# Placing matmul operands modulo 256 bytes, and key-span copies on GpSimd instead of VectorE

## The chip, the cores and the metric

The kernel runs on one core of one Trainium2 chip. The metric is the device time of one execution in microseconds. PE is TensorE's matmul side and PEld its weight load, DVE is VectorE, ACT is ScalarE, POOL is GpSimd, and SP is the engine that issues most DMAs.

## The reference

Three parts follow each other. Chunked attention: 4 batches, 8 heads, 768 tokens, head size 64; each chunk of 32 queries sees 8 memory keys and a span of 56 keys around it. Then a top-1 mixture of 8 experts (512 to 1024 to 512) over the 3072 tokens, and then a dense SiLU layer (512 to 2048 to 512).

```python
k_full = np.concatenate([mem_k, k_ctx], axis=2)          # 8 + up to 56 keys
scores = scale * np.matmul(q_c, k_full.transpose(0, 1, 3, 2))
a = np.exp(scores)                                       # scores less their row maximum
a = a / (np.sum(a, axis=-1, keepdims=True) + 1e-09)
out[:, :, c_start:c_end] = np.matmul(a, v_full)
...
expert_idx = np.argmax(logits, axis=1)
h = np.maximum(x[mask] @ w1[e], 0.0)
out[mask] = gate_w[mask, None] * (h @ w2[e])
...
h = x @ w_in
g = h * (1.0 / (1.0 + np.exp(-h)))
return (g @ w_out).astype(np.float32)
```

## The kernel before

**Products.** Expert and dense products run on the fp32r type, each operand split into a high and a low tile, so one product is three matmuls (`three`, lines 94 to 98): high times high, high times low, low times high. In each, one operand is loaded into the array as 128 columns (stationary; its load shows as PEld) and the other streams past it (moving, 256, 384 or 512 columns). While one matmul streams, the weights of the next are loaded.

**Attention** runs over 16 pairs of heads in 32 units of half a pair each (loop from line 895). A unit `u` has, on PE, the scores of unit u (24 matmuls of 32 x 128), the transposes of the exponents of u-1 (`turned`), the transposes of the output of u-3 (`columns`), and the values of u-2 (24 matmuls of 32 x 130). On DVE it has the row maximum (`mx`, line 795), the subtraction (`e`, line 798), the key spans of one head (line 714), and the division (`den` at 832 and 834, `xb` at 836). ACT has the exponentials, three copies, and squares. Between these, one step at a time, DVE takes the steps of a routing generator (`advance`, lines 296 to 330). Each engine works its instructions in the order in which they are written.

The key spans are what `windows(j, h, part)` writes: it lays the 56-key span of each of 12 chunks out in `kbuf[j % 2]` (64 partitions, 12 x 56 elements, line 714), and the 8 memory keys beside them (12 x 8 elements, line 715). Head 0 of a pair goes on ACT, head 1 on DVE; the memory keys go on POOL from pair 3 on. The scores of pair j wait for them. Pair 0 is laid out ahead of the loop, pair j+1 while pair j is worked on. POOL begins with fills of buffers and, at line 276 to 290, the constants of the routing (`routing_constants`), and these are written ahead of the first unit.

**Slots.** Tokens of one expert are worked on in slots: two leading slots of two tiles of 128 tokens (`pre`), up to four of three tiles (`threes`), and then as many of two tiles as there are (`twos`). For each of 8 column blocks of the expert, `first_mm` does 12 matmuls with w1 stationary and the slot's x moving (256 columns for two tiles, 384 for three), and `second_mm` does 3 matmuls for each tile, with h stationary and the block of w2 (called v2, 512 columns) moving. The leading slots have their x and h in the small space (tiles `xhs`, `hhs`), all others in the large space (`xhl`, `xhm`, `hhl`). In this run 3 three-tile and 8 two-tile slots are taken after the leading two.

**Dense layer.** Six groups of 512 tokens, 16 column blocks each. `up` does 12 matmuls with w_in stationary and the group's y moving; `add` does 12 with the gated g stationary and w_out moving. The weights of blocks 0 to 5 are in `w2a`, of 6 to 15 in `w2b`, both as high and low tiles. Groups 0, 2, 4 have y in `yh`, `yl`; groups 1, 3, 5 in `yh1`, `yl1`. The profile leaves numbers out of names, so `yh` stands for both.

**Places.** Pools are stacked from both ends of a partition's memory. The built program gives these start addresses, modulo 256 bytes (all inner offsets that the matmuls use are multiples of 256 bytes):

| tiles | before | after |
|---|---|---|
| expert weights w1, v2 | 224 | 224 |
| x, h of the small space | 160 | 160 |
| x, h of the large space | 224 | 160 |
| w2a | 160 | 224 |
| w2b, g, y of groups 1, 3, 5 | 224 | 224 |
| y of groups 0, 2, 4 | 128 | 224 |

Of the kernel before, what the change touches and what calls it, by code (L numbers as in the profile page):

```python
# [10 lines left out]
F32 = mybir.dt.float32  # L11
F32R = mybir.dt.float32r
# [10 lines left out]
P = 128  # L23
# [10 lines left out]
DM = H * D  # L34
KD = DM // P
# [11 lines left out]
N2 = (N - 2 * SLOT - NE) // SLOT + NE  # L47
SURE2 = (NTC - 3 * N3 + 1) // 2
NA = 2 * N2

LEAST = 2.0 ** -15

# [5 lines left out]
def tile_chunk_attention_top1_moe_silu_mlp(ctx, tc, qT, kT, vW, emb, tau, wm, wo, out, dbg=None):  # L58
    nc = tc.nc
    wo = wo.bitcast(I32)  # L60
    PE, ACT, DVE, POOL, SP = nc.tensor, nc.scalar, nc.vector, nc.gpsimd, nc.sync
# [8 lines left out]
    gd = dram.tile([N, 1], F32, name="gd")  # L70
    td = dram.tile([NA * P, 1], I32, name="td")
    bank = [psum.tile([P, DM], F32, name=f"bank{i}") for i in range(8)]
# [5 lines left out]
    d = const.tile(full, F32, name="d")  # L78
# [5 lines left out]
    rows3_i = const.tile([P, 3 * (N3 + 1)], I32, name="rows3_i")  # L84
    rows2_i = const.tile([P, NA], I32, name="rows2_i")
    chosen_i = const.tile([1, 2], I32, name="chosen_i")
# [143 lines left out]
    seg = rp.tile([P, NE, NT], F32, name="seg")  # L230
    tiles = rp.tile([P, 1, NA], F32, name="tiles")
    mx = rp.tile([P, NT, 1], F32, name="r_mx")
# [29 lines left out]
    wideh = rp.tile([P, NTC, 2 * NE], F32, name="wideh")  # L262
    ahf = rp.tile([P, NT, NA], BF16, name="ahf")
    ah = rp.tile([P, NT, 2, NA], BF16, name="ah")
    ixs = rp.tile([P, NA + 3 * N3], F32, name="ixs")
    ixp = rp.tile([P, NA], F32, name="ixp")
# [414 lines left out]
    with ExitStack() as a:  # L681
# [26 lines left out]
        def windows(j, h, part):  # L708
            rows = slice(h * D, h * D + D)
            half = slice(part * (NCH // 2), (part + 1) * (NCH // 2))  # L710
            src, dst = kraw[j][rows], kbuf[j % 2][rows, h, half]
            copy = DVE.tensor_copy if h else ACT.copy
            w = src[:, NMEM + half.start * CH:]
            copy(dst[:, :, NMEM:], bass.AP(tensor=w.tensor, offset=w.offset, ap=[w.ap[0], [CH, NCH // 2], [1, WIN]]))
            (POOL.tensor_copy if j > 2 else copy)(
                dst[:, :, 0:NMEM], src[:, 0:NMEM].unsqueeze(1).to_broadcast([D, NCH // 2, NMEM])
            )
# [36 lines left out]
        for part in range(2):  # L754
            for h in range(2):
                windows(0, h, part)
# [139 lines left out]
        for u in range(NU + 2):  # L896
# [12 lines left out]
            if ahead < NJ:  # L909
                windows(ahead, 1, u % 2)  # L910
                windows(ahead, 0, u % 2)
                advance()
# [48 lines left out]
    lg = ex.enter_context(tc.tile_pool(name="lg", bufs=1, side="right"))  # L961
    large = [space(lg, "l", 3)]
    large.append(dict(large[0], x=tuple(lg.tile([P, KD, 3 * P], F32R, name=f"x{n}m") for n in "hl")))
    yfirst = [lg.tile([P, 2, DM], F32, name=f"yfirst{n}") for n in range(2)]
    w2d = tuple(lg.tile([P, DM], F32R, name=f"v2{n}3") for n in "hl")
    for n, s in enumerate(order):
        s.y = lambda n=n: yfirst[n] if n < 2 else ymore[:, 0:order[n].nt]
# [18 lines left out]
                advance(pe=True)  # L986
    rt.close()
    ypool = ctx.enter_context(tc.tile_pool(name="ypool", bufs=1))
    ymore = ypool.tile([P, 4, DM], F32, name="ymore")
    POOL.memset(ymore, 0.0)  # L990


# [9 lines left out]
    GT2 = TG * P  # L1002
    NG = NT // TG
    yrow = ctx.enter_context(tc.tile_pool(name="yrow", bufs=1))
    yr = [y[:, c] for y in yfirst for c in range(2)]
    tok_i = [yrow.tile([P, TG], I32, name=f"tok{g}") if g else pre_i for g in range(NG)]
    gt = [yrow.tile([P, TG], F32, name=f"gt{i}") for i in range(2)]
    yt = [tuple(yrow.tile([P, KD, GT2], F32R, name=n) for n in ("yh", "yl"))]

    dx = ctx.enter_context(ExitStack())  # L1010
    dp = dx.enter_context(tc.tile_pool(name="dp", bufs=1))
# [87 lines left out]
    j = 0  # L1099
# [13 lines left out]
    for s in plan:  # L1113
        for at, do in sorted(plan[s], key=lambda p: p[0]):
            f = int(at)
# [25 lines left out]
    with ExitStack() as a:  # L1141
# [73 lines left out]
        for i in range(NI2):  # L1215
            g, f = steps[i]
            j = NB2 + i
# [89 lines left out]
```

## Time and profile before

| | us |
|---|---|
| median of 3 runs (1033.83 to 1038.53) | 1034.95 |
| the profiled execution | 1034.16 |
| its span, first to last instruction | 1032.2 |
| PE busy | 985.2 (95%) |
| PEld busy | 822.4 (80%) |
| DVE busy | 613.6 (59%) |
| ACT busy | 463.2 (45%) |
| POOL busy | 168.6 (16%) |

The stages are read from the first matmul of each: attention up to about 115 us, the slots to 474 us, the dense layer to the end. A matmul's duration in the timeline is modelled and overlaps its neighbour's; the distance of two starts is the time that one really takes up. The chain of waits of this profile holds only the last output transfer and is of no use here.

### The profile page before, as it was taken

The numbers are of one execution on the slowest core, as the hardware profiler recorded it, in microseconds if no ns is written. First come the engines' busy times: TensorE is split into PE (matmuls) and PEld (weight loads), VectorE is DVE, ScalarE is ACT, GpSimd is POOL, SyncE is SP. The second block draws the span as 40 slices with busy tenths as digits, with TensorE's granted clock in tenths as the row PEclk, the third lists the DMA queues.
The fourth block names the chain that finished last, engine by engine and source line by source line (L and its number), as shares of the span: only waits on it lengthen the run. The fifth ranks groups of instructions, "written<-read, shape, count | busy, mean of one in ns | idle before, by whom it ended". The sixth has DMA issues, their size and how long they took to land. (4 is left out here: it accounts for less than half of the span.)

```text
span 1032.2 us, 16833 instructions
## 1 busy us (share of the span) xinstructions
PE 985.2 (95%) x6366; PEld 822.4 (80%) x6366; DVE 613.6 (59%) x1225; ACT 463.2 (45%) x890; POOL 168.6 (16%) x225
## 2 busy tenths in 40 slices
PE   6888888999999999998999999999999999999998
PEld 4666677999888999997778888878887888788886
DVE  8999797677777887896899942422232232223221
ACT  8886555445456565664544333222321331232221
POOL 5133032011020000002230002050023005001001
PEclk9999999999999999999999999999999999999999
DMA  8986756566488887776343201020011002000001
GB/s 302 341 316 231 244 196 208 196 216 224 130 272 255 273 276 256 253 242 191 95 124 100 82 1 41 19 64 1 1 52 30 1 4 79 1 1 31 10 1 41
DMA packets 44213, 139.37 MB, mean 135 GB/s; under 512 B 6422, under 2 KB 6480, under 8 KB 44120
## 3 DMA queue, kind: packets, MB, share of 16 engines
q1 hardware_dynamic: 36632, 118.22, 33.7%
q0 software_dynamic: 7488, 19.95, 6.4%
q8 instruction: 53, 0.87, 0.4%
q14 instruction: 40, 0.33, 0.1%
HBM read 115.32 MB, written 22.84 MB: 134 GB/s over the span
## 5 line engine op out<-in xcount | busy, mean ns | idle before, releaser
L1169 DVE TENSOR_TENSOR sg<-bank,sg 128x512 f32<-128x512 f32 x96 | 66.2, 690 | 235.9 <-ACT sg L1164 235.9
L1164 ACT ACTIVATE sg<-bank 128x512 f32<-128x512 f32 x96 | 57.4, 598 | 277.7 <-PE bank L98 244.2
L96 PE MATMUL bank<-yh,w2bh 128*128 128x512 f32 x240 | 95.0, 396 | 0.0
L92 DVE TENSOR_TENSOR gl<-sg,gh 128x512 fp32r<-128x512 f32 x92 | 63.8, 693 | 52.5 <-ACT gh L91 48.5
L98 PE MATMUL bank<-yh,w2bl 128*128 128x512 f32 x240 | 94.5, 394 | 0.0
L97 PE MATMUL bank<-yl,w2bh 128*128 128x512 f32 x240 | 94.3, 393 | 0.0
L97 PE MATMUL bank<-w2bl,gh 128*128 128x512 f32 x224 | 87.4, 390 | 0.0
L96 PE MATMUL bank<-w2bh,gh 128*128 128x512 f32 x224 | 87.4, 390 | 0.0
L98 PE MATMUL bank<-w2bh,gl 128*128 128x512 f32 x224 | 87.4, 390 | 0.0
L91 ACT CAST gh<-sg 128x512 fp32r<-128x512 f32 x92 | 57.1, 621 | 64.8 <-DVE sg L1169 60.9
L1192 POOL DMA_INDIRECT out_dram<-o,tok x20 | 20.4, 1022 | 389.0 <-DVE o L1189 348.4
L181 ACT ACTIVATE hhl<-bank 128x256 fp32r<-128x256 f32 (+1 forms) x88 | 36.3, 413 | 101.0 <-PE bank L98 95.2
L96 PE MATMUL bank<-v2h,hhl 128*128 128x512 f32 x200 | 80.4, 402 | 0.0
L97 PE MATMUL bank<-v2l,hhl 128*128 128x512 f32 x200 | 78.9, 394 | 0.0
L98 PE MATMUL bank<-v2h,hll 128*128 128x512 f32 x200 | 78.5, 393 | 0.0
L92 DVE TENSOR_TENSOR w1l<-raw,w1h 128x512 fp32r<-128x512 f32 x106 | 72.9, 687 | 8.4 <-ACT w1h L91 5.3
L92 DVE TENSOR_TENSOR v2l<-raw,v2h 128x512 fp32r<-128x512 f32 x106 | 72.9, 688 | 0.0
L182 DVE SCALAR_TENSOR_TENSOR hll<-bank,hhl 128x256 fp32r<-128x256 f32 (+1 forms) x88 | 40.3, 458 | 54.6 <-ACT hhl L181 53.7
L147 POOL DMA_INDIRECT xrowl<-xd,rows_i x28 | 31.0, 1108 | 243.1 <-PE bank L169 201.2
L97 PE MATMUL bank<-xll,w1h 128*128 128x256 f32 (+1 forms) x224 | 68.5, 306 | 2.1 <-DVE xll L92 2.1
L96 PE MATMUL bank<-xhl,w1h 128*128 128x256 f32 (+1 forms) x224 | 68.7, 307 | 1.4 <-DVEq L1134 1.4
L98 PE MATMUL bank<-xhl,w1l 128*128 128x256 f32 (+1 forms) x224 | 68.7, 306 | 0.2 <-DVE w1l L92 0.2
(308 smaller groups left out, 2426.9 us busy)
## 6 DMA issues: line engine op xcount, KB each, us to landing
raw<-in_wm_dram SPq DMA_DIRECT2D x109, 512.0 KB
coded<-in_wo_dram SPq DMA_DIRECT2D x36, 512.0 KB
vbuf<-in_vW_dram SPq DMA_DIRECT2D x32, 390.0 KB
k<-in_kT_dram SPq DMA_DIRECT2D x16, 400.0 KB
q<-in_qT_dram SPq DMA_DIRECT2D x16, 384.0 KB
xd<-xb SPq DMA_DIRECT2D x8, 768.0 KB
ys<-ymore SPq DMA_DIRECT2D x8, 512.0 KB
ys<-yfirst SPq DMA_DIRECT2D x7, 512.0 KB
```

The source lines that it names most:

```text
L91: ACT.copy(hi, src)
L92: eng.tensor_tensor(lo, src, hi.bitcast(F32), op=ALU.subtract)
L96: PE.matmul(out, lhsT=lh, rhs=rh, start=start, stop=False)
L97: PE.matmul(out, lhsT=lh, rhs=rl, start=False, stop=False)
L98: PE.matmul(out, lhsT=ll, rhs=rh, start=False, stop=stop)
L147: POOL.indirect_dma_start(out=s.where["row"][:, c], out_offset=None, in_=xd[0:LEAD * P] if s in pre else xd, in_offset=IndirectOffsetOnAxi ...
L181: ACT.activation(hh, h, AF.Relu)
L182: DVE.scalar_tensor_tensor(hl, h, 0.0, hh.bitcast(F32), op0=ALU.max, op1=ALU.subtract)
L1164: ACT.activation(sg, h, AF.Sigmoid)
L1169: DVE.tensor_tensor(sg, h, sg, op=ALU.mult)
L1192: POOL.indirect_dma_start(out=out, out_offset=IndirectOffsetOnAxis(ap=tok_i[g][:, c:c + 1], axis=0), in_=o, in_offset=None,)
```

## The change

Three edits go to where tiles lie, one to which engine does a copy.

- `yfirst0` gets 16 more columns (64 bytes) than it uses. It lies above the large space in a pool that is stacked downward, so the large space's x, h and gather tiles move 64 bytes down.
- `ymore` gets 64 bytes more as well, and `yt[0]` (`yh`, `yl`) is allocated ahead of the small tiles `tok` and `gt` instead of behind them. This moves `w2a` by 64 bytes and `yh`, `yl` to the end of `w2a`. The table above has the result.
- In `windows`, head 1 of pairs 1 to 15 goes to POOL in place of DVE: 30 copies of 64 x 12 x 56, and 4 of 64 x 12 x 8 for pairs 1 and 2. Pair 0 stays on DVE.

```diff
--- before.py
+++ after.py
@@ -47,6 +47,8 @@
 N2 = (N - 2 * SLOT - NE) // SLOT + NE
 SURE2 = (NTC - 3 * N3 + 1) // 2
 NA = 2 * N2
+
+HOME = 16
 
 LEAST = 2.0 ** -15
 
@@ -709,7 +711,7 @@
             rows = slice(h * D, h * D + D)
             half = slice(part * (NCH // 2), (part + 1) * (NCH // 2))
             src, dst = kraw[j][rows], kbuf[j % 2][rows, h, half]
-            copy = DVE.tensor_copy if h else ACT.copy
+            copy = (POOL.tensor_copy if j else DVE.tensor_copy) if h else ACT.copy
             w = src[:, NMEM + half.start * CH:]
             copy(dst[:, :, NMEM:], bass.AP(tensor=w.tensor, offset=w.offset, ap=[w.ap[0], [CH, NCH // 2], [1, WIN]]))
             (POOL.tensor_copy if j > 2 else copy)(
@@ -961,7 +963,10 @@
     lg = ex.enter_context(tc.tile_pool(name="lg", bufs=1, side="right"))
     large = [space(lg, "l", 3)]
     large.append(dict(large[0], x=tuple(lg.tile([P, KD, 3 * P], F32R, name=f"x{n}m") for n in "hl")))
-    yfirst = [lg.tile([P, 2, DM], F32, name=f"yfirst{n}") for n in range(2)]
+    yfirst = [
+        lg.tile([P, 2 * DM + HOME * (1 - n)], F32, name=f"yfirst{n}")[:, 0:2 * DM].rearrange("p (c d) -> p c d", c=2)
+        for n in range(2)
+    ]
     w2d = tuple(lg.tile([P, DM], F32R, name=f"v2{n}3") for n in "hl")
     for n, s in enumerate(order):
         s.y = lambda n=n: yfirst[n] if n < 2 else ymore[:, 0:order[n].nt]
@@ -986,7 +991,7 @@
                 advance(pe=True)
     rt.close()
     ypool = ctx.enter_context(tc.tile_pool(name="ypool", bufs=1))
-    ymore = ypool.tile([P, 4, DM], F32, name="ymore")
+    ymore = ypool.tile([P, 4 * DM + HOME], F32, name="ymore")[:, 0:4 * DM].rearrange("p (c d) -> p c d", c=4)
     POOL.memset(ymore, 0.0)
 
 
@@ -1002,10 +1007,10 @@
     GT2 = TG * P
     NG = NT // TG
     yrow = ctx.enter_context(tc.tile_pool(name="yrow", bufs=1))
+    yt = [tuple(yrow.tile([P, KD, GT2], F32R, name=n) for n in ("yh", "yl"))]
     yr = [y[:, c] for y in yfirst for c in range(2)]
     tok_i = [yrow.tile([P, TG], I32, name=f"tok{g}") if g else pre_i for g in range(NG)]
     gt = [yrow.tile([P, TG], F32, name=f"gt{i}") for i in range(2)]
-    yt = [tuple(yrow.tile([P, KD, GT2], F32R, name=n) for n in ("yh", "yl"))]
 
     dx = ctx.enter_context(ExitStack())
     dp = dx.enter_context(tc.tile_pool(name="dp", bufs=1))
```

The order of PE, ACT and SP is the same as before. Two places on the others:

POOL, from its last constant to the first spans of the attention loop; `kbuf1`, `k3` are the spans and keys of pair 3 (odd pairs use `kbuf1`). Before:

```order
L289 MEMSET hot_132 128x192
L290 MEMSET ixs_179 128x46
L715 COPY kbuf1_204<-k3_316 64x12x8 x4
L715 COPY kbuf0_203<-k4_412 64x12x8 x4
L715 COPY kbuf1_204<-k5_516 64x12x8 x4
```

After:

```order
L291 MEMSET hot_132 128x192
L292 MEMSET ixs_179 128x46
L716 COPY kbuf1_204<-k1_222 64x12x56
L717 COPY kbuf1_204<-k1_222 64x12x8
L716 COPY kbuf1_204<-k1_222 64x12x56
L717 COPY kbuf1_204<-k1_222 64x12x8
L716 COPY kbuf0_203<-k2_239 64x12x56
L717 COPY kbuf0_203<-k2_239 64x12x8
```

The spans of pairs 1 and 2 now stand behind the constants in POOL's order.

DVE, units 12 and 13 of the attention; `mx12` is the row maximum of unit 12, `den10` the divisor of unit 10. Before:

```order
L795 TENSOR_REDUCE mx12_860<-bank0_69 128x6
L798 TENSOR_TENSOR e12_862<-bank0_69,mx12_860 128x3x2x64
L303 SCALAR_TENSOR_TENSOR r_v_130<-d_83,down_126 128x48
L714 COPY kbuf1_204<-k7_722 64x12x56
L832 TENSOR_SCALAR den10_892<-bank4_73 128x6
L305 TENSOR_REDUCE r_mv_131<-r_v_130 128x6
L834 RECIPROCAL den10_892<-den10_892 128x6
```

After:

```order
L797 TENSOR_REDUCE mx12_860<-bank0_69 128x6
L800 TENSOR_TENSOR e12_862<-bank0_69,mx12_860 128x3x2x64
L305 SCALAR_TENSOR_TENSOR r_v_130<-d_83,down_126 128x48
L834 TENSOR_SCALAR den10_892<-bank4_73 128x6
L307 TENSOR_REDUCE r_mv_131<-r_v_130 128x6
L836 RECIPROCAL den10_892<-den10_892 128x6
```

The copy between `e` and `den` is gone, and nothing else has moved.

## Rows read from the trace of the kernel before

**Rows 1.** stages: us, busy PE, PEld, DVE, ACT, POOL, PEclk, DMA, GB/s
```profile
20.00:100.00 80.00, 70.01 (x1478) 52.99 (x1476) 72.71 (x206) 62.95 (x138) 22.39 (x61) 1.00 0.87 306
115.00:474.00 359.00, 347.89 (x2144) 311.87 (x2142) 283.36 (x587) 207.16 (x423) 46.04 (x45) 1.00 0.69 228
474.00:1032.00 558.00, 544.40 (x2384) 441.07 (x2384) 230.07 (x369) 169.25 (x286) 82.63 (x84) 1.00 0.13 41
```

**Rows 2.** timeline, PE, dense: start us, us, engine, line, operation, tiles
```profile
770.63 0.39 PE L96 MATMUL bank<-w2ah,gh 128*128 128x512 f32 x1
...
773.43 0.40 PE L96 MATMUL bank<-yh,w2ah 128*128 128x512 f32 x1
...
794.97 0.39 PE L96 MATMUL bank<-w2bh,gh 128*128 128x512 f32 x1
...
797.69 0.39 PE L96 MATMUL bank<-yh,w2bh 128*128 128x512 f32 x1
...
900.76 0.40 PE L96 MATMUL bank<-yh,w2bh 128*128 128x512 f32 x1
...
903.57 0.39 PE L96 MATMUL bank<-w2bh,gh 128*128 128x512 f32 x1
```

**Rows 3.** timeline of PE, two-tile slots: a small-space one, then a large-space one
```profile
133.92 0.28 PE L96 MATMUL bank<-xhs,w1h 128*128 128x256 f32 x1
...
135.29 0.39 PE L96 MATMUL bank<-v2h,hhs 128*128 128x512 f32 x1
...
136.67 0.28 PE L96 MATMUL bank<-xhs,w1h 128*128 128x256 f32 x1
...
338.06 0.28 PE L96 MATMUL bank<-xhl,w1h 128*128 128x256 f32 x1
...
339.49 0.40 PE L96 MATMUL bank<-v2h,hhl 128*128 128x512 f32 x1
...
340.89 0.60 PE L1081 MATMUL bank<-ident,yfirst 128*128 128x128 f32 x4
```

**Rows 4.** timeline of PE, a three-tile slot
```profile
234.43 0.33 PE L96 MATMUL bank<-xhl,w1h 128*128 128x384 f32 x1
...
236.54 0.39 PE L96 MATMUL bank<-v2h,hhl 128*128 128x512 f32 x1
```

**Rows 5.** groups by line, PE, 174:474 us: xcount, busy us, mean ns
```profile
L96 PE MATMUL bank<-v2h,hhl 128*128 128x512 f32 x200 | 80.4, 402 | 0.0
...
L98 PE MATMUL bank<-xhl,w1l 128*128 128x384 f32 x96 | 32.4, 337 | 0.0
```

**Rows 6.** timeline of PE and DVE, one attention unit without a routing step
```profile
28.30 0.87 PE L821 MATMUL bank<-vbuf,et 128*32 128x130 f32 x24
28.33 0.56 DVE L798 TENSOR_TENSOR e<-bank,mx 128x384 f32<-128x384 f32 x1
...
28.92 0.51 DVE L714 COPY kbuf<-k 64x672 f32<-64x672 f32 x1
...
29.46 0.16 DVE L832 TENSOR_SCALAR den<-bank 128x6 f32<-128x6 f32 x1
```

**Rows 7.** waits, 10:112 us: who, for whom, us in total, times, longest
```profile
DVE den L832 <- PE bank L821: 4.0, 7, 1.8
```

**Rows 8.** timeline of DVE, an attention unit with a routing step
```profile
47.91 0.51 DVE L714 COPY kbuf<-k 64x672 f32<-64x672 f32 x1
48.45 0.17 DVE L832 TENSOR_SCALAR den<-bank 128x6 f32<-128x6 f32 x1
```

**Rows 9.** timeline of DVE and POOL, units 2 and 30, and POOL's last constant
```profile
13.97 0.56 DVE L795 TENSOR_REDUCE mx<-bank 128x6 f32<-128x384 f32 x1
...
14.47 0.14 POOL L290 MEMSET ixs<- 128x46 f32 x1
...
101.70 0.54 DVE L795 TENSOR_REDUCE mx<-bank 128x6 f32<-128x384 f32 x1
```

**Rows 10.** groups by line, POOL, whole span: xcount, busy us, mean ns
```profile
L281 POOL COPY row<-token 128x1 f32<-128x1 f32 x1 | 0.2, 184 | 0.1
...
L715 POOL COPY kbuf<-k 64x96 f32<-64x96 f32 x52 | 14.5, 279 | 45.6 <-DMA k<-in_kT_dram 22.5 <-PE bank L809 9.5 <-PE bank L821 4.3
```

## The prediction, made before the changed kernel ran

> **What bounds the kernel now.** I read the stages first [rows 1]. From 115 us on PE is busy 348 of 359 us in the slots and 544 of 558 in the dense layer, while DVE has 79% and 41%, at a granted clock of 1.00. What makes one matmul shorter there shortens the run by as much. In the attention (20 to 100 us) DVE has 72.7 of 80 us (91%), PE 70.0, ACT 62.9 and POOL 22.4: DVE sets the pace, and POOL has room.
>
> A busy PE is not PE at its peak, so I then read distances of starts in the timeline. All of these are runs of 12 (or 6) matmuls with nothing in between.
>
> - Dense, `add` on w2a: 770.63 to 773.43, 2.80 us for 12, **233.3 ns** each. `add` on w2b, 24 us later, same shape, same g: 794.97 to 797.69, **226.7 ns**. `up` with y of group 4 (`yh`) on w2b: 900.76 to 903.57, 234.2 ns [rows 2]. By the table of places, the operands of the 226.7 run lie 0 bytes apart modulo 256, those of the others 64 and 96.
> - Slots of two tiles, 256 columns: in the small space (x 64 bytes off w1) 133.92 to 135.29, **114.2 ns**; in the large space (in line) 338.06 to 339.49, **119.2 ns**. Their second layer, six of 512 columns: 230.0 off line, 233.3 in line [rows 3].
> - Three tiles, 384 columns, in line: 234.43 to 236.54, 175.8 ns [rows 4].
>
> So the trace holds the experiment already: distance modulo 256 goes with the pitch, 0 is best for the long runs at 512 columns, and 64 off is better at 256. The change gives each stage the relation that was the quicker one in these rows.
>
> **Dense layer.** All pairs come to 0 bytes apart, at the same remainder (224) as w2b and g have now, so I take 226.7 for all. Counts by the code: 6 groups x 12 matmuls x 6 or 10 blocks, `add` the same.
> - `add` on w2a: 432 x (233.3 - 226.7) = 2.85 us.
> - `up` on w2b, groups 0, 2, 4: 360 x 6.8 (the row gives 7.5, other runs of this class a little less) = 2.45.
> - `up` on w2a: 432 matmuls, 32 or 192 bytes off. No row here; bounded by 0 and by 6.6 each. The groups with `yh` behave as the row above (216 x 6.2 = 1.35), for the others I take 4.5 (0.95).
> - `add` on w2b after an off-line `up` starts slower than after an in-line one; half a us over 672 matmuls, and 48 last ones that read weights out of `yh`, 0.3.
>
> Sum **-8.2 us**, bounds -6.5 and -9. PE waits for nothing that this would uncover: DVE has 41% there.
>
> **Slots.** The large space comes into the relation of the small one. With 200 second-layer matmuls a term, 72 of them from the three slots of three tiles (96 first-layer ones are 32 a slot), eight slots of two tiles follow [rows 5].
> - First layer, 256 columns: 8 x 96 = 768 x (119.2 - 114.2) = 3.8 us. A run begins slower than it ends, and some runs of the small space lie nearer 115.5, so I take 4 ns: 3.1. Bounds 1.5 and 5.
> - Second layer of these: 384 x (233.3 - 230.0) = 1.3; I take 0.9. That of the three-tile slots (216) I leave at 0.2. Bounds +0.6 and -2.2 together.
> - 384 columns have no row off line. From below, the gain of the nearest row (5.0 ns, same tiles, 256 columns): 288 x 5.0 = 1.4. From above, a loss such as 64 bytes make at 512 columns (6.6 ns): 1.9. I take -0.6, nearer to the row that shares its tiles.
>
> Sum **-4.8 us**, bounds 0 and -8. DVE rises from 79% to about 80% there and stays behind PE.
>
> **Attention, what DVE loses.** 30 copies of 0.51 us. What lies beside them is the values on PE: `den` waits for both.
> - In a unit without a routing step `e` ends at 28.89, the copy stands at 28.92 to 29.43, `den` at 29.46; PE's values end at 29.17 [rows 6]. Without the copy `den` can start at about 29.24: 0.22 us a unit, and PE's values are late next.
> - Seven times `den` waits for PE's values already [rows 7]: 0 there.
> - Where a routing step stands ahead, `den` comes straight behind the copy, 47.91 to 48.45, with the values long done: the whole 0.5 [rows 8].
>
> Of the 28 copies in units 2 to 29 (told apart by the distance of their `mx` rows, the ends of which are in [rows 9]), 7 give 0, eleven stand in units without a routing step (2.4 us), ten behind one (5.0): **-7.4 us**.
>
> **Attention, what POOL gets.** The nearest rows are 279 ns for 96 elements in 12 runs and 184 ns for 1 [rows 10]: 0.99 ns an element beyond 0.18, so 672 cost 0.85 us. All of the 279 ns as per-element cost would give 1.95, the upper end. With two copies of memory keys POOL then has 1.4 us a unit (2.5 at the upper end) against 3.13 us that a unit takes ((101.70 - 13.97) / 28 [rows 9]). Its share rises, but it stays ahead. In its queue the copies now stand among the routing's `bh` steps, which wait for DVE; the spans are written two units before their use, which covers that. SP's loads of keys now wait for POOL in place of DVE, for a copy that is done two units earlier.
>
> What is not covered is the start. POOL finishes its constants at 14.61 [rows 9], and pair 1 now waits in line behind them. Its first span is done at 14.61 + 0.85 + 0.28 = 15.74, the 24 matmuls of unit 2's scores take some 0.87 (the values' row has that many [rows 6]), so unit 2's `mx` comes at 16.6 to 16.7 and not at 13.97. PE stands idle before it, and the next unit's scores want the second half behind another 1.1 us. I take **+3.0 us**, with ends 2.2 and 4.5 (POOL at its upper price).
>
> Attention together **-4.4 us**, bounds +1 and -8.
>
> **Sum.** 1034.16 (profiled) - 8.2 - 4.8 - 4.4 = 1016.8; the median lies 0.8 above the profiled run, so 1017.5. I say **1017.5 us**.
>
> **Rivals.**
> 1. *The places are not the cause.* Then w2a would be slow for another reason, and only the attention's 4.4 us remain: 1030.5. For it: the off-line dense runs differ among themselves by 2 to 4 ns, so more than the remainder acts. Against it: w2b is quick with g and slow with `yh` in neighbouring runs [rows 2], so it is the pair and not the tile. The Trainium skill ("TensorE: Matmul & The Clock Gate", Step-by-step: what each phase is for) has TensorE read moving operand and weights through two independent ports, so that loading the next weights takes nothing from the running matmul; by that rule no address would matter and this rival's time would come out. The 233.3 and 226.7 ns of one shape speak against it. Chance 0.06.
> 2. *The attention gives nothing.* The start costs 4.5 and PE's values (24 matmuls each) hold the loop, so that units without a routing step gain nothing: 0 to +2 instead of -4.4, 1022 to 1024. For it: PE has 70 of 80 us in the stage [rows 1]. Chance 0.15.
> 3. *Slower.* POOL becomes the attention's bound. A unit costs POOL the copy plus 0.56; with 3.13 us a unit now, it decides from a copy of 2.6 us on, and eats the 13 us of the other stages from about 2.85. At 3.0 us: 27 units x 0.43 + 4.5 at the start + 3 = +19, so 1035 - 13 + 19 = 1041. It would need 4.2 ns an element where the rows have 1 to 2.9. Chance 0.03.
>
> The forecast keeps 0.76.
>
> **How the numbers follow.** Ends of the forecast's own terms: attention -8 to +1, slots -8 to 0, dense -9 to -6.5; all at one end is unlikely, so about 1011 to 1024 for forecast and rival 2. With a little of rival 1's side the range is **1011 to 1025**. About 0.5% (5.2 us) is what a measurement can tell from no change. Faster by more: forecast, rival 2: 0.91. Within: rival 1, 0.06. Slower: 0.03.
>
> **What would show it.** Dense runs of `add` on w2a and `up` with any y at 227 ns. Two-tile slots' first layer at 114 to 116 ns. POOL's span copies at 0.8 to 0.9 us, DVE at some 82% of the attention in place of 91; unit 2's `mx` near 16.7; units without a routing step 0.2 us shorter, with `den` waiting for PE's values; the first expert matmul at about 111 us, not 115. I would be wrong if the 256-column pitch stayed at 119 or rose, if 384 columns rose above 178, or if the first expert matmul came at 115 or later.

## The result, and the profile after

The changed kernel takes **1025.97 us** (median, 1024.18 to 1030.07), the kernel before beside it 1035.08 us: ratio **0.9912, 95% interval 0.9894 to 0.9931**. The forecast was 1017.5 us in a range of 1011 to 1025, so the direction was right and half of the gain was missing. The same two kernels on other chips give another ratio, **0.9841 (0.9828 to 0.9854)**: 1024.00 us before, 1007.09 us after, almost all of the 17.4 us (8.2 + 4.8 + 4.4) that had been forecast. So two things have to be explained, why the sum was right there and what took some 8 us away here. In what follows A is the chip of the result, B to G are the chips of the experiments in their order (A and B may be the same one).

Profiled on A, the changed kernel took 1027.44 us, with a span of 1025.7. First the stages, as in [rows 1], moved with the earlier ends (us, busy PE, PEld, DVE, ACT, POOL, granted clock, DMA share, GB/s):

```profile
20.00:100.00 80.00, 74.19 (x1539) 56.96 (x1537) 62.39 (x191) 63.82 (x142) 38.45 (x87) 0.98 0.86 307
113.00:469.00 356.00, 345.39 (x2143) 310.23 (x2141) 282.92 (x587) 207.21 (x422) 46.00 (x45) 1.00 0.69 230
469.00:1026.00 557.00, 539.72 (x2384) 442.90 (x2384) 230.43 (x369) 169.72 (x286) 82.98 (x84) 0.99 0.13 41
```

DVE has come down from 91% to 78% of the attention (62.39 of 80 us) and POOL risen to 48%. But in the dense layer PE is busy for 4.7 us less while the stretch has hardly become shorter (557 in place of 558 us): PE stands still more.

The pitches that the forecast rests on all came. The timeline of PE on A, one `add` on w2a, one `up` of an even group on w2b, then a three-tile and a two-tile slot (start, us, engine, line, operation, tiles), which answer to [rows 2 to 4]:

```profile
770.21 0.39 PE L98 MATMUL bank<-w2ah,gh 128*128 128x512 f32 x1
...
772.93 0.39 PE L98 MATMUL bank<-yh,w2ah 128*128 128x512 f32 x1
...
896.05 0.39 PE L98 MATMUL bank<-yh,w2bh 128*128 128x512 f32 x1
...
898.77 0.39 PE L98 MATMUL bank<-w2bh,gh 128*128 128x512 f32 x1
```
```profile
228.70 0.34 PE L98 MATMUL bank<-xhl,w1h 128*128 128x384 f32 x1
...
230.78 0.39 PE L98 MATMUL bank<-v2h,hhl 128*128 128x512 f32 x1
...
332.85 0.28 PE L98 MATMUL bank<-xhl,w1h 128*128 128x256 f32 x1
...
334.23 0.39 PE L98 MATMUL bank<-v2h,hhl 128*128 128x512 f32 x1
```

Both dense runs take 2.72 us for 12, 226.7 ns each (233.3 and 234.2 before). 384 columns take 173.3 ns (175.8), 256 columns 115.0 (119.2).

The attention on A: unit 2, the last constant on POOL and the first span copy behind it, `mx` of two neighbouring units without a routing step (kernel before, then the changed one), and two rows of the waits from 10 to 110 us (who, for whom, us in total, times, longest), beside [rows 6, 7, 9]:

```profile
16.88 0.56 DVE L797 TENSOR_REDUCE mx<-bank 128x6 f32<-128x384 f32 x1 [5.26 <-PE bank L788]
```
```profile
14.09 0.14 POOL L292 MEMSET ixs<- 128x46 f32 x1
14.29 0.75 POOL L716 COPY kbuf<-k 64x672 f32<-64x672 f32 x1
```
```profile
27.68 0.55 DVE L795 TENSOR_REDUCE mx<-bank 128x6 f32<-128x384 f32 x1
30.36 0.55 DVE L795 TENSOR_REDUCE mx<-bank 128x6 f32<-128x384 f32 x1
```
```profile
27.49 0.55 DVE L797 TENSOR_REDUCE mx<-bank 128x6 f32<-128x384 f32 x1
29.95 0.55 DVE L797 TENSOR_REDUCE mx<-bank 128x6 f32<-128x384 f32 x1
```
```profile
DVE den L834 <- PE bank L823: 13.3, 22, 1.8
...
PE bank L788 <- issue: 2.0, 1, 2.0
```

POOL copies a span in 0.75 us, unit 2 begins at 16.88 us, a unit without a routing step takes 2.46 us in place of 2.68, and `den` now waits 22 times for PE's values where it waited 7 times. The last row is new and was not foreseen: once, at 54.23 us, PE stood for 2.0 us in the middle of a unit's scores, and the profile shows nothing that it waited for. Units 15 and 16 took 4.82 and 3.86 us in place of some 2.5, the second of them for the most part at a granted clock of 0.5.

Now the missing part. In the rows that follow, `gh` is the high half of the gated g that ACT makes for `add`; `held` is the copy of group 0's first sums, which frees the banks for group 1; `give` scatters a group's output rows, and `pick` and `pick_gate` gather the rows, tokens and gates of the next group, four of each. Waits of PE in the dense layer, kernel before and then the changed one (480 to 1030 us):

```profile
PE bank L96 <- ACT gh L91: 4.2, 3, 1.6
PE bank L96 <- ACT held L1184: 1.6, 1, 1.6
```
```profile
PE bank L98 <- ACT gh L93: 6.7, 3, 2.3
PE bank L98 <- ACT held L1189: 1.8, 1, 1.8
PE bank L98 <- issue: 0.5, 1, 0.5
```

These waits were there before, and they have grown. Each of the three on `gh` stands ahead of the `add` of block 5 of groups 2, 3 and 4; the one on `held` is the fourth. One of them in the changed kernel, first ACT, then PE, then POOL (the bracket is the idle time ahead of the row, and what ended it):

```profile
688.05 0.60 ACT L1169 ACTIVATE sg<-bank 128x512 f32<-128x512 f32 x1 [9.01 <-PE bank L100]
689.41 0.62 ACT L93 CAST gh<-sg 128x512 fp32r<-128x512 f32 x1 [0.76 <-DVE sg L1174]
```
```profile
690.08 0.50 PE L98 MATMUL bank<-w2ah,gh 128*128 128x512 f32 x1 [2.23 <-ACT gh L93]
```
```profile
669.49 0.97 POOL L1197 DMA_INDIRECT out_dram<-o,pre_i  x1 [2.52 <-DVE gl L94]
670.76 0.99 POOL L1058 DMA_INDIRECT ymore<-ys,rows_i  x1 [0.30 <-issue]
672.05 0.96 POOL L1064 DMA_INDIRECT tok<-td,rows_i  x1 [0.30 <-issue]
...
683.40 0.94 POOL L1072 DMA_INDIRECT gt<-gd,tok  x1 [0.30 <-issue]
684.65 0.94 POOL L1072 DMA_INDIRECT gt<-gd,tok  x1 [0.30 <-issue]
```

The sigmoid at 688.05 needs only the `up` that PE had ended at 682.41. ACT stood 9.01 us all the same. The trace also records when semaphores change, and there the cause is seen. PE raises one semaphore at the end of each `up` and each `add`:

```
chip A, changed kernel          chip D, changed kernel (same place in the program)
end on PE   update seen         end on PE   update seen
671.53      671.54              661.35      661.36
679.69      681.58              669.51      669.52
682.41      687.97              672.23      672.24
685.13      688.10              674.95      674.96
687.85      688.22              677.67      677.68
694.94      694.96              680.39      680.40
```

(Some updates have no record on A; rows whose update has none there are left out on both sides.) The sigmoids tell the same without these records: of the 96, the median starts 0.10 us behind the end of its `up`, but those of block 5 in groups 2, 3 and 4 start 5.6 to 5.7 us behind it on A, while on D none is more than 0.35 us late. On A, PE's updates come late while POOL is deep in a run of twelve gathers back to back (0.30 us between two), and come all at once 2.4 us after the last of them ends (684.65 + 0.94 = 685.59). Kernel before, same place, the last gather of POOL and the sigmoid of ACT:

```profile
690.97 0.94 POOL L1067 DMA_INDIRECT gt<-gd,tok  x1 [0.30 <-issue]
```
```profile
694.33 0.60 ACT L1164 ACTIVATE sg<-bank 128x512 f32<-128x512 f32 x1 [8.36 <-remote]
```

The gather ends at 691.91, the sigmoid starts 2.42 us later. I call this the **held updates**. The place of the run of gathers is fixed by the end of the group before (the four scatters of `give`, then `pick`, `pick_gate`), not by how fast PE works through the blocks behind it. So a quicker PE only arrives earlier at the wait: `up` and `add` of one block take 5.44 us in place of some 5.6, which is 0.8 us over five blocks, and the three waits on `gh` grew by 0.97, 0.71 and 0.84 us (by the distances of starts beyond the pitch, which come out some 0.16 us longer than the rows of waits).

### The profile page after: what moved, and what is told of

Its sections match the earlier page's. It is cut to its first block, busy times and chain, and to the rows that moved or that the text cites. A ratio compares the mean times of both kernels' runs of the same rounds, so it can differ in the third digit from the quotient of the medians.

```text
span 1025.7 us, 16830 instructions
## 1 busy us (share of the span) xinstructions
PE 978.3 (95%) x6366; PEld 823.4 (80%) x6366; DVE 596.8 (58%) x1191; ACT 462.5 (45%) x890; POOL 188.8 (18%) x259
```

## The experiments

**Each part alone** (chip B, kernel before 1033.45 us). The edits are the three pieces of the change:

```diff
 att_only
-            copy = DVE.tensor_copy if h else ACT.copy
+            copy = (POOL.tensor_copy if j else DVE.tensor_copy) if h else ACT.copy
 slots_only
-    yfirst = [lg.tile([P, 2, DM], F32, name=f"yfirst{n}") for n in range(2)]
+    yfirst = [lg.tile([P, 2 * DM + HOME * (1 - n)], F32, ...) for n in range(2)]
 dense_only
+    ymore = ypool.tile([P, 4 * DM + HOME], F32, name="ymore")...    # and yt ahead of yr
```

> The kernel before with the third part of the change alone: GpSimd copies the second head's key spans from the second pair of heads on; every tile stays where it was. Parts add up (the prediction's term): attention -4.4 us, so 1030.6. Theory of the accident: the changed kernel's attention was 2.2 us shorter instead of 4.4 only because TensorE stood 2.0 us at 54 us for nothing that the profile shows and ran at half clock behind it; if that does not come again here, attention is 4.5 to 5.5 us shorter and the time 1029.5 to 1030.5; if the stop belongs to the copies on GpSimd, it comes again and the time is 1032 to 1033. First scores' maximum of unit 2 near 16.9 us in each case.

> The kernel before with the 64 bytes ahead of the second half of yfirst alone: x and h of the 384-column slots start at 160 modulo 256 instead of 224, dense tiles and attention stay. Parts add up: 256-column pitch 119.3 to 115.6 ns, 384 columns 175.5 to 173.5 ns, in sum -3.9 us of pitches, time 1031 to 1031.5. If the changed kernel's 2.7 us instead of 4.8 in this stage were a wait that grows as the pitch shrinks, the waits of the stage are longer by over 1 us here too; if it was the half-clock spell at 175.8 us alone, they stay within 0.5 us of before unless a spell falls there.

> The kernel before with w2a, yh and yl moved to 224 modulo 256 alone. Prediction's term: -8.2 us, 1026.8. Theory of the held updates (TensorE's semaphore updates do not reach the other engines while GpSimd issues its run of twelve gathers, so the add of block 5 of each group starts at a time that GpSimd sets): the pitches fall by 7.7 us, the four waits in front of an add behind the gathers rise from 1.4 to 1.7 us to 2.0 to 2.4 us, in sum about 3 us, which leaves -4.7 us, 1030.3; with a half-clock spell of 1.6 us behind one or two of the waits up to 1033.5. Rival (the wait was an accident of one execution): waits as before, 1026.8 to 1027.5.

| kernel | median us | ratio to before (95%) |
|---|---|---|
| att_only | 1030.14 | 0.9973 (0.9960 to 0.9986) |
| slots_only | 1030.87 | 0.9971 (0.9958 to 0.9984) |
| dense_only | 1031.39 | 0.9983 (0.9974 to 0.9993) |

Together -8.0 us of the 9.1 on A: the parts add up within their intervals, and it is the dense part that is far too small, 2.1 us of 8.2. In slots_only the waits of PE in the slots did not grow (8.2 us in its trace, 9.4 in the kernel before on A), so nothing takes that gain back by waiting. The trace of dense_only has the new pitches and these waits, with two half-clock stretches behind them:

```profile
PE bank L98 <- ACT gh L93: 6.2, 3, 2.1
PE bank L98 <- DVE held L1186: 1.8, 1, 1.8
```

The held updates expected 1030.3 and up to 1033.5, the accident 1026.8 to 1027.5: the first holds. In att_only the stop at 54 us did not come again (units 15 and 16 took 2.67 and 2.31 us), and the first expert matmul stands at 109.68 us in place of 113.04: the stop does not belong to the copies on POOL, and what made it is not known. The gain of att_only in the median, 3.3 us, is still less than its trace shows, 5.5 us up to the first expert matmul (the profiled execution was among the quickest, 1024.85 us, with one of the four waits absent); that difference stays open.

**The gathers spaced** (chip B). Ahead of each `pick`, POOL fills the row block that the gather then overwrites:

```diff
     def pick(g, c):
         t = (g - 1) * TG + c
+        for _ in range(4 if g > 1 else 2):
+            POOL.memset(yr[c], 0.0)
```

> The changed kernel with four (for group 1: two) memsets on GpSimd of the row block ahead of each pair of gathers, about 2 us of other GpSimd work, so that the twelve gathers do not come back to back. Nothing else is moved. Theory of the held updates: TensorE's updates arrive on time, the four waits of 1.97, 2.38, 2.42 and 2.38 us in front of an add fall to under 0.5 us each, and with them the half-clock spells behind them go: 7 to 11 us less than the changed kernel, 1015 to 1019. Rival (ScalarE's delay has another cause that only ends at the same time, such as its own instructions arriving late): the waits stay, 1025 to 1027. Rival (the later end of the gathers sets the wait): the waits grow by some 8 us each, 1050.

**1010.59 us** (0.9781, 0.9768 to 0.9795), against the changed kernel's ratio of 0.9912 on A: some 13.5 us more. POOL's timeline and then the only wait of PE that is left from 480 us on:

```profile
664.94 2.30 POOL L1059 MEMSET ymore<- 128x512 f32 x4
667.51 0.99 POOL L1060 DMA_INDIRECT ymore<-ys,rows_i  x1 [0.27 <-POOL ymore L1059]
668.80 0.96 POOL L1066 DMA_INDIRECT tok<-td,rows_i  x1 [0.30 <-issue]
669.76 2.29 POOL L1059 MEMSET ymore<- 128x512 f32 x4
```
```profile
PE bank L98 <- ACT sg L1171: 0.9, 1, 0.9
```

From 480 us on no recorded update of PE's semaphore is late there (seven ends have no record), and no sigmoid starts more than 0.71 us behind its `up`, against 5.5 us in dense_only, though POOL does 39 us more work. Against dense_only on the same chip (547.6 us from the first dense `up` to the last matmul) the dense layer takes 534.5. Of these 13.1 us most are the four waits (8.7, of which 1.1 is left) and the two half-clock stretches behind them (some 3). That ACT was late for a reason of its own is ruled out by this run. The time is below the 1015 to 1019 expected.

**Spacing in the kernel before, and the tiles in line with spacing** (chip C, kernel before 1023.84 us).

> The kernel before with the same memsets of 2.3 us on GpSimd ahead of each pair of gathers (half as many for group 1); all tiles and copies as before. Theory of the held updates: the four waits of 1.73, 1.41, 1.71 and 1.54 us in front of an add fall to 0 to 1.1 us, so 5 to 6.5 us less than the kernel before, 1027 to 1028.5 on a chip where that takes 1033.5; no more than that, since the pitches of TensorE stay. Rival (spacing is only worth something together with the moved tiles): within 1 us of before.

> The kernel before with the dense tiles in line and the spaced gathers, no moved slots, copies as before. Theory of the held updates: what the tiles in line save in pitch, 7.7 us, now shows in full against the kernel with the spaced gathers alone, where it was 2.1 us without the spacing: 1019 to 1021. Rival (the tiles in line give some 2 us whatever the gathers do): 1025 to 1026.

before_spaced took 1024.52 us, 1.0007 (0.9998 to 1.0016): nothing, where 5 to 6.5 us were expected. The reason is the chip: the kernel before itself is 10 us quicker here, and no trace of C shows a late update. dense_spaced took 1017.54 us, 0.9941, so the tiles in line give 7.0 us in the median (dense layer 540.5 to 532.9 us), near the 7.7 expected; its absolute range was set for a slower chip.

**A block of fills ahead of the run** (chip C), meant as the control for spaced: the same kind of work, the run unbroken.

```diff
+        if c == 0 and g > 1:
+            for k in range(9):
+                POOL.memset(yr[k % TG], 0.0)
```

> The changed kernel with nine memsets in one block (5.2 us) ahead of the first gather of groups 2 to 5, and the twelve gathers back to back behind them. Theory of the held updates: the run of gathers, and with it the end of the hold, moves back by about one add with its up (5.45 us), so the wait stays at 1.8 to 2.4 us but stands in front of the add of block 6 instead of 5: 1024 to 1027. Rival (any GpSimd work of that kind, or any later gathers, takes the wait away): waits under 0.5 us and 1015 to 1019.

> The changed kernel with nine memsets of GpSimd (4.3 us) in one block ahead of the first gather of groups 2 to 5 and the twelve gathers back to back behind them. On a chip that holds TensorE's updates (the kernel before takes 1033 to 1035 us there): if the back-to-back run makes the hold, the waits ahead of an add stay at 1.0 to 2.4 us, one block of the loop later, and the time is 1021 to 1027; if any GpSimd work ahead of the gathers takes the hold away, they are gone and it is near the spaced kernel's 1010.6. On a chip that does not hold them (1024 us): 1009 to 1012, and nothing is told apart.

On C it took 1011.38 us, with no wait but one of 1.1 us, although twelve gathers come back to back. The waits are gone, as the rival expected, but for neither theory's reason: the chip doesn't hold updates. The same kernel took 1009.98 us on D, 1012.36 on E and 1011.18 on F, always on chips that take 1024 us for the kernel before; before_spaced took 1.0004 on D and 1.0011 on E. So **the control was never run on a chip that holds updates**. That it is the unbroken run, and not any gather without other work ahead of it, rests on spaced and on the table above: with indirect DMAs 3.5 us apart (the scatters of `give`) the updates are on time, and the first late one falls into the eighth gather of the run (due 679.69, in a run that began at 670.76).

**Both kernels again** (chip D).

> The changed kernel, nothing edited. The kernel before took 1033 to 1035 us on two chips and 1024 us on a third, where the traces of four kernels show no late update of TensorE's semaphore although twelve gathers came back to back in one of them. Theory: whether updates are held behind a run of gathers belongs to the chip. On a chip that holds them the ratio is near 0.991 again, with waits of 2.0 to 2.4 us ahead of the add of block 5; on one that does not, the waits are absent, the pitches' 7.7 us show in full, and the change gives 13 to 16 us, ratio 0.985 to 0.987. Rival: the chip changes all parts alike and the ratio stays at 0.991.

> The kernel before, nothing edited, for its trace on the same chip. On a chip that holds updates: waits of 1.4 to 1.7 us ahead of four adds, 1033 to 1035 us. On one that does not: none of these waits, every update of TensorE's semaphore within 0.1 us of the end of its matmul behind the gathers, 1024 us.

> The changed kernel, nothing edited. On a chip that holds updates: ratio 0.990 to 0.993 to the kernel before, waits of 2.0 to 2.4 us. On one that does not: ratio 0.983 to 0.986, no such waits.

After 1007.09, before 1024.00: **0.9841**. On E it was 1007.67 against 1023.80, 0.9842 (0.9820 to 0.9866). One of the four waits does come without a late update: on `held`, after_3 has 1.7 us on E and before_spaced_3 1.6. So only the three on `gh` are shown to be the held updates' work. ACT of the changed kernel on D, beside the last gathers of POOL, at the place shown for A:

```profile
666.89 0.60 ACT L1169 ACTIVATE sg<-bank 128x512 f32<-128x512 f32 x1 [3.46 <-PE bank L100]
672.33 0.60 ACT L1169 ACTIVATE sg<-bank 128x512 f32<-128x512 f32 x1 [3.46 <-PE bank L100]
```
```profile
670.71 0.95 POOL L1072 DMA_INDIRECT gt<-gd,tok  x1 [0.30 <-issue]
671.96 0.94 POOL L1072 DMA_INDIRECT gt<-gd,tok  x1 [0.30 <-issue]
```

The same instructions in the same order, the gathers back to back, and at this place ACT never waits longer than 3.47 us. The dense stretch of before and after on D (same columns as the stages above):

```profile
474.00:1022.00 548.00, 541.85 (x2384) 441.81 (x2384) 230.17 (x368) 169.16 (x286) 83.17 (x84) 0.99 0.13 42
```
```profile
466.00:1004.00 538.00, 532.29 (x2384) 440.33 (x2384) 229.89 (x368) 170.44 (x286) 83.78 (x84) 1.00 0.13 43
```

**Where the start of the attention goes** (chip C): POOL's copies from the third pair on.

```diff
+            copy = (POOL.tensor_copy if j > 1 else DVE.tensor_copy) if h else ACT.copy
```

> The changed kernel with the spaced gathers, and GpSimd's copies only from the third pair of heads on, VectorE copying for the second as before. If the 2.9 us by which unit 2 of attention starts later are the queue on GpSimd at the start (its memsets and the routing's constants ahead of the second pair's copies), unit 2's maximum comes back from 16.8 to between 14 and 15.3 us and the time falls by 1.5 to 2.9 us against the spaced kernel, 1007.5 to 1009. Rival (the first loads set it): 16.8 stays, 1010.6.

> The changed kernel with spaced gathers and VectorE copying for the second pair of heads too: 1003 to 1008 us on either kind of chip, since nothing is left in it that the hold could lengthen; ratio 0.970 to 0.977 on a chip that holds updates, 0.981 to 0.985 on one that does not.

1005.81 us (0.9827), and unit 2 is back at 13.99 us, which settles the cause of the later start:

```profile
13.99 0.56 DVE L797 TENSOR_REDUCE mx<-bank 128x6 f32<-128x384 f32 x1
```

The time lies below the 1007.5 to 1009 expected, which were set from spaced on B; spaced itself was not run on C. On E, beside the changed kernel's 1007.67, it took 1006.11 us (0.9817, 0.9798 to 0.9835): ahead of it, but with intervals that overlap. It was not run on a chip that holds updates; there spaced, at 1010.59, is the best that was run, and beats both kernels by far.

**Distance or place** (chip G, kernel before 1024.52 us): yh and yl of the even groups at 160, with w2a at 160, everything else as before, and the block of fills of one_block.

```diff
+    yt = [tuple(yrow.tile([P, KD, GT2], F32R, name=n) for n in ("yh", "yl"))]    # ahead of tok_i, gt
     yr = [y[:, c] for y in yfirst for c in range(2)]
```

> Two edits of the kernel before that are read in different rows. First, yh and yl of the even groups start at 160 modulo 256, where w2a starts too, instead of 128; w2b, g and the odd groups stay at 224. If the distance between the two operands sets the pitch, the up of the even groups on w2a (216 matmuls) falls from 233 to 227 ns, and every other kind stays: add on w2a 233 ns, up on w2b of the even groups 233 to 234 ns, up on w2a of the odd groups 230 to 231 ns; in sum 1.3 us. If the place 224 itself mattered, no kind falls. Second, nine memsets in one block ahead of the first gather of groups 2 to 5, the twelve gathers back to back behind them. On a chip that holds TensorE's updates (the kernel before takes 1033 to 1035 us): waits of 1 to 2.4 us ahead of an add behind each run if the run makes the hold, none if any GpSimd work ahead of it takes the hold away. On one that does not (1024 us): no such wait, and 1022 to 1023.5.

1023.30 us, 0.9987 (0.9978 to 0.9997). One `up` on w2a of an even group in the kernel before, then the same with the `add` behind it in this run:

```profile
680.94 0.40 PE L96 MATMUL bank<-yh,w2ah 128*128 128x512 f32 x1
...
683.74 0.40 PE L96 MATMUL bank<-w2ah,gh 128*128 128x512 f32 x1
```

```profile
675.27 0.39 PE L96 MATMUL bank<-yh,w2ah 128*128 128x512 f32 x1
675.97 0.39 PE L96 MATMUL bank<-yh,w2ah 128*128 128x512 f32 x1
676.66 0.39 PE L96 MATMUL bank<-yh,w2ah 128*128 128x512 f32 x1
677.34 0.39 PE L96 MATMUL bank<-yh,w2ah 128*128 128x512 f32 x1
678.02 0.40 PE L96 MATMUL bank<-w2ah,gh 128*128 128x512 f32 x1
...
680.82 0.39 PE L96 MATMUL bank<-yh,w2ah 128*128 128x512 f32 x1
```

The `up` of before, 32 bytes off line, took 2.80 us for 12, 233.3 ns each. Here the steps of three are 0.70, 0.69, 0.68 and 0.68 us: the run in line starts at 233 ns, as the off-line `add` ahead of it ended, and comes down to 227 (229.2 over the 12, so about two thirds of the 6.6 ns expected); the `add` (64 bytes off) stays at 233.3. The other kinds stayed as well: `up` on w2b of the even groups at 233.3 ns in the median (233.8 before), `up` on w2a of the odd groups at 230.4 (230.3). So the distance of the two operands counts, at another place than 224 too. The Trainium skill ("TensorE: Matmul & The Clock Gate", Step-by-step: what each phase is for) gives moving operand and weights two independent ports; by that no address would matter. The rows differ with the address, and they decide. The chip didn't hold updates, so the other edit told nothing.

## Why the prediction was wrong, step by step

- **"All pairs come to 0 bytes apart, so I take 226.7 for all": right.** On D the dense layer, first `up` to last matmul, went from 541.46 to 532.54 us, -8.9 for a forecast of -8.2 (1.5 of it is a half-clock stretch that only the kernel before had, and a wait of 0.6 on `held` that only the changed kernel had goes the other way). The terms as they stand in the prediction come to 8.4, not 8.2. On A the pitches fell by 7.7 us.
- **"PE waits for nothing that this would uncover: DVE has 41% there": this step failed.** It was argued from a share of another engine, and PE's own waits in this stage weren't read. They stand in the trace of before: 4.2 us behind ACT's gh and 1.6 behind `held`. Asking what ended them would have led to ACT's sigmoid (8.36 us idle, ended by nothing that the profile names) and to POOL's gathers beside it. On A the four waits grew from 6.4 to 9.2 us (distances of starts beyond the pitch; the one on `held` by 0.25 of it), because the gain in the first five blocks of a group only brings PE earlier to a point that POOL sets; a fifth wait grew by 0.3, and two half-clock stretches behind the longer waits cost some 1.5 us each. Together 6.1 us, which leaves 1.6 of 7.7: 549.96 to 548.35 us.
- **Slots, -4.8: right in kind, too large.** On D -3.7: the 768 matmuls of 256 columns gave 3.0 (forecast 3.1), the second layer 0.6 (1.1), the 384 columns 0.4 (0.6). The unknown sign at 384 columns was taken rightly. On A a half-clock stretch at 175.8 us took 1.7 of it. That stretch is no accident of the changed kernel: 15 of the 20 traces have one behind the same wait, and the kernel before on A is among the five without.
- **Attention, -4.4: right in kind, a little small.** The later start came as worked out, 16.88 us against 16.6 to 16.7, and POOL's copy costs 0.75 us, estimated 0.85. Units without a routing step went from 2.68 to 2.46 us, the 0.22 forecast. First expert matmul on D 115.07 to 109.76, -5.3: with 2.8 for the later start, the copies taken from DVE gave 8.1 us where I had 7.4. On A the stop at 54 us took some 3.3.
- **The sum.** On D the span falls by 17.9 us and the median by 16.9, for a forecast of 17.4. On A the span falls by 6.5. By stages the 11.4 us between them are 7.3 in the dense layer, 3.2 in the attention, 1.0 in the slots. Some 6 us are the longer waits with what follows them; the rest, the stop at 54 us and half-clock stretches that one trace of a pair has and the other has not, is luck of the traces compared. The medians differ by less, 16.9 - 9.1 = 7.8 us.
- **The rivals.** Neither places, nor a worthless attention, nor a bound on POOL came true. The mechanism that did was not among them, although it is of the first kind to look for: a wait that takes up what is saved.

## What to carry to other kernels

Before a gain on the busiest engine is counted in full, read that engine's own waits in the same stage and ask of each what sets its end; where another engine's queue does, what is saved ahead of it comes back as wait. Break long runs of indirect DMAs on GpSimd with other work where TensorE's results are wanted meanwhile: it cost the kernel before up to 1.4 us on chips that didn't need it and gave the changed one some 13.5 on one that did. And place the operands of long fp32r matmul runs 0 bytes apart modulo 256 at 512 columns, 64 apart at 256 and 384, by measured pitch; the short runs of 512 columns behind those in the slots were quicker 64 apart as well (229.2 against 231.3 ns in the median on D).

## What the runs showed of the hardware that I had not expected

- **Chips differ by what they hold.** The kernel before took 1035.08 and 1033.45 us on A and B, and 1023.84, 1024.00, 1023.80, 1024.72 and 1024.52 on C to G. On A and B the profile has 589 to 595 update records of PE's semaphore for 607 ends, on the others 610 or 611. On A and B records of DVE's and ACT's semaphores are missing too (1119 for 1159 ends and 828 for 856 in the changed kernel on A), none of POOL's, but none of those on record came late in the dense layer. Late updates come only on chips with lost records, but not with every loss: spaced has 595 records and, in the dense layer, no late one. Whether the chip or something else in those sessions makes the difference, what carries the updates, and whether they would be late with no profile being taken, no run here shows.
- **A wait of two microseconds can cost more than itself.** In the changed kernel on A the wait that ended at 690.08 us is followed by a stretch at half the clock, 1.2 of 2.4 GHz (stretch, length, busy PE, PEld, DVE, ACT, POOL, granted clock):

```profile
660.00:687.00 27.00, 27.00 (x120) 22.34 (x119) 5.94 (x9) 4.88 (x8) 14.41 (x15) 1.00 0.26 79
691.20:694.50 3.30, 3.30 (x9) 2.53 (x8) 0.84 (x2) 0.62 (x1) 0.00 (x0) 0.50 0.00 0
```

  PE was busy without a break ahead of it, then stood 2.38 us. Of the three waits of that length two were followed by such a stretch, the third was not, and in the kernel before none of the 1.4 to 1.7 us was. In the slots every one of the 20 traces has a wait of 2.1 to 2.3 us between 168 and 179 us, and 15 of them have such a stretch within 1.6 us behind its end.
- **A run in line needs a few matmuls to reach its pitch** when an off-line run is ahead of it (0.70 us for the first three, 0.68 for the later ones).
